# FNet block with a gated MLP on one core: 1.8 MB transfers in halves, y operand sums a pair ahead, the first y unit in a row

## The chip, the core and the metric

The kernel runs on one core of a Trainium2 chip. Its engines are TensorE (PE: matmuls; PEld: loading of their weights), VectorE (DVE), ScalarE (ACT), GpSimd (POOL) and SyncE (SP), which here only issues transfers. The metric is the time on the device in microseconds (us), lower is better.

## The reference

The input x is 2048 x 512, all in float32.

```
xn  = (x - mean) / sqrt(var + 1e-5)                 # per row
a   = xn @ Dre.T ;  b = xn @ Dim.T                  # 512 x 512 each
s   = Sre @ a - Sim @ b                             # 2048 x 2048 each
h   = relu(xn @ w1 + b1) ** 2                       # 512 -> 1792
g   = silu(h @ w2 + b2)                             # 1792 -> 512
out = x + s * g
```

## The kernel before

**Products.** Each float32 operand is split into a high and a low part: ScalarE makes the high part by a rounding copy (L124), VectorE subtracts it from the source to get the low part (L127). A product is three passes, high x high, high x low, low x high. Most matrix products are done by a Strassen-Winograd scheme: of 2 x 2 blocks, sums of blocks are made by VectorE (`sums_b`, `sums_a`, L256 to L268), seven block products numbered 1 to 7 are made on TensorE, and their results are combined. So an operand goes through three stages: load, sums, split.

**Stages, in order.** The order is written out by hand; every engine runs its instructions in that order, and a program-wide tool adds the waits.

1. Layer norm and two chunks (c = 0, 1) of the sequence transform in plain form.
2. Chunks c = 2 to 7 of the sequence transform, 8 steps j each, called "m" (L324). A step takes 42 matmuls of 128 x 256. Its tile u of the transform matrix (512 KB) is loaded four steps ahead into one of three buffers, summed two steps ahead and split one step ahead. The result of a chunk is put together by `combine` (eight "closing" operations, L305) around the start of the next chunk and stored to memory as `pqd`.
3. Y: eight units u = 0 to 7 of 84 matmuls (L702 with operands `wdp`, `yg`), which finish s. Unit u takes the y operands 2u and 2u + 1 (loaded from `pqd`, summed at L262 to L265, split) and the four hidden-transform operands `wdp`. A unit has four PSUM regions A to D. Products 1, 7, 6, 2 of unit u stand between products 5, 4, 3 of unit u - 1. `seed` copies a region to another (ScalarE), `m7`, `c11`, `c12` are ScalarE's copies of results and `c22` (L712), `c21` (L715) VectorE's; `c12` also stores the unit's result y from ScalarE's queue (L741).
4. H: 28 units of 42 matmuls (L702 with `xT`, `w`) of the first MLP product, and O: the second (L808), with the end.

**Side work.** Operands that later stages need are made beside the stages, by generators that advance one stage per call: `go("d2")` runs the next part of d2. Letters: d and v build the hidden-transform and the first two W1 operands and store them (1792 KB each, `wdd` and `w1d`, L375); p loads `wdd` back (L418), k loads `w1d` back (L628); y makes the first y operands 0 to 2; x makes the transposed normalised x (`xT`); m loads rows of the statistics; V, w make further MLP operands; h the operands of O. The tables EARLY (chunk, step), Y_SIDE (unit, two places) and H_SIDE (unit, three places) say where each call stands.

**Queues.** Nearly all loads and the large stores are issued by SP, in program order. An SP instruction that waits for a buffer holds the ones behind it.

The loop of stage 3 before:

```
for u in range(NC):
    n = 2 * u + 3
    ...
    y_sums(n)              # operand 2u+3: the second of unit u+1
    unit.products(1)
    ...
    y_split(n)
    y_load(n + 3)
    ...
    y_sums(n + 1)          # operand 2u+4: the first of unit u+2
    ...
    y_split(n + 1)
    y_load(n + 4)
```

Of the kernel before, what the change touches and what calls it, by code (L numbers as in the profile page):

```python
# [8 lines left out]
F32 = mybir.dt.float32  # L9
# [9 lines left out]
NC = S // CW  # L19
# [20 lines left out]
}  # L40


Y_SIDE = (
    ((), ()),
    (("x0",), ()),
    (("x0",), ()),
    (("x0",), ()),
    (("x0",), ("k0",)),
    (("x1",), ("V2", "V3", "k1")),
    (("x1", "x1", "m1"), ("x1", "V2", "x2")),  # L50
    (("x0", "x0", "V4", "x1", "x1", "V3"), ("x2",)),
)


# [3 lines left out]
    2: (("x2",), ("V4",), ("V6",)),  # L58
    3: (("V5",), ("V5",), ()),
    4: (("V6",), ("V6",), ("w4",)),  # L60
    5: (("x3", "m2"), ("x2",), ("x4",)),
    6: (("x3",), ("x3",), ("x5",)),
    7: (("w4",), ("w4",), ("w5",)),
    8: (("x4",), (), ()),
    9: (("x4",), ("x4",), ("x6",)),
    10: (("w5",), ("w5",), ("w0",)),
    11: (("x5", "m3"), (), ()),
    12: (("x5",), ("x5",), ("x7",)),
    13: (("w0",), ("w0",), ("w1",)),
    14: (("x6",), (), ()),  # L70
    15: (("x6",), ("x6",), ()),
    16: (("x7",), (), ()),
    17: (("x7",), ("x7",), ("h0", "h1")),
    20: (("h0",), (), ()),
    21: (("h1",), (), ()),
# [11 lines left out]
HI, LO = 0, 1  # L87
# [31 lines left out]
def fnet_gated_kernel(ctx, tc, x, xt, ct, wd, w1, w2, b1, b2, out):  # L119
    nc = tc.nc  # L120
    ctx.enter_context(tc.manual_schedule(engines=None))

    def split_hi(hi, lo, src):
        nc.scalar.activation(hi, src, AF.Copy)  # L124

    def split_lo(hi, lo, src):
        nc.vector.tensor_tensor(lo, src, hi.bitcast(F32), op=ALU.subtract)  # L127

    def split(*parts):
        split_hi(*parts)  # L130
        split_lo(*parts)

    def copy(to, src, scale=1.0):
        nc.scalar.activation(to, src, AF.Copy, scale=scale)  # L134
# [12 lines left out]
    PQD = [dram.tile([P, 2, 4, 256], F32, name=f"pqd{c}") for c in range(NC)]  # L147
    WDD = [dram.tile([P, 2, 7, 256], F32, name=f"wdd{n}") for n in range(ND)]
    W1D = {p: dram.tile([P, 2, 7, 256], F32, name=f"w1d{p}") for p in W1_EARLY}
# [8 lines left out]
    def buf(tag, shape, name, dtype=F32):  # L158
        bufs = {"u": 3, "bn": 3, "sm": 3}.get(tag, 1)
        return pool.tile(shape, dtype, tag=tag, bufs=bufs, name=name)  # L160
# [80 lines left out]
    def load_c(c, j, hs=slice(0, 2)):  # L241
        if (c, j) not in raw:
            raw[c, j] = buf("u", [P, 8, CW], f"u{c}_{j}")
        q = slice(2 * hs.start, 2 * hs.stop)
        nc.sync.dma_start(raw[c, j][:, q], ct[c, j, :, q])
# [31 lines left out]
    def step_load(n):  # L277
        if n < len(steps):
            load_c(*steps[n])
        elif n - len(steps) + YFIRST < 2 * 3:  # L280
            y_load(n - len(steps) + YFIRST)

    def step_sums(n):
# [31 lines left out]
    def some(steps_, n):  # L315
        for _ in range(n):
            next(steps_)
# [26 lines left out]
    steps = [(c, j) for c in range(PLAIN, NC) for j in range(NJ)]  # L344
# [3 lines left out]
    def go(*names):  # L348


        for v in names:
            if v[0] == "h" and int(v[1:]) >= NTC * NP:
                continue
            if v not in making:
                making[v] = makers[v[0]](int(v[1:]))
            next(making[v])

    def weight(n, raw_, sums_, to, k, e=None, turn=False):

        if e:  # L360
            e = buf(e, [P, 8, 256], f"{n}rt")
            r, t = e[:, 0:4], e[:, 4:8]
        else:
            r, t = buf(f"pq{k}0", [P, 4, 256], f"{n}r"), buf(f"pq{k}1", [P, 4, 256], f"{n}t")
        nc.sync.dma_start(r, raw_)
        yield
        if turn:
            copy(r[:, I22:I21 + 1], r[:, I22:I21 + 1], -1.0)
        sums_(t, r)
        yield  # L370
        g = buf(f"wd{k}", [P, 2, 7, 256], f"{n}g", F32R)
        split(g[:, HI, 0:3], g[:, LO, 0:3], r[:, 1:4])
        yield
        split(g[:, HI, 3:7], g[:, LO, 3:7], t)
        nc.sync.dma_start(to, g.bitcast(F32))  # L375
        yield

    makers["d"] = lambda n: weight(f"wd{n}", wd[n], sums_b, WDD[n], n % 2, "e" if n == 1 else None, True)
    makers["v"] = lambda n: weight(f"w1{n}", w1[n], sums_w1, W1D[n], n % 2)
# [1 line left out]
    def load_pq(n, x_):  # L381
        nc.sync.dma_start(x_, PQD[n // 2][:, n % 2])

    Y_HOME = ("xc2", "xc3"), ("xc4", "xc5"), ("xc6", "xc7")
    YFIRST = 3
    yop, yraw, WDP = {}, {}, []

    def y_load(n):
        if n < 2 * NC:
            yraw[n] = buf("u", [P, 8, 256], f"yraw{n}")  # L390
            load_pq(n, yraw[n][:, 4:8])

    def y_sums(n):
        if n < 2 * NC:
            sums_rows(yraw[n], yraw[n][:, 4:8], True)

    def y_split(n):
        if n < 2 * NC:
            g = yop[n] = buf(Y_HOME[n // 2 % 3][n % 2], [P, 2, 7, 256], f"yg{n}", F32R)
            split(g[:, HI], g[:, LO], yraw[n][:, 0:7])  # L400
# [14 lines left out]

    def load_wd(n):
        t = buf(("wd0", "wd1", "xc0", "xc1")[n], [P, 2, 7, 256], f"wdp{n}", F32R)
        nc.sync.dma_start(t.bitcast(F32), WDD[n])  # L418
        WDP.append(t)
        yield  # L420

    makers["y"] = y_early
    makers["p"] = load_wd
# [32 lines left out]
    g = plain_parts(0, 1)  # L456
# [7 lines left out]
    for j in range(1, NJ):  # L464
# [15 lines left out]
        g = plain_parts(*order[j + 1])  # L480
# [61 lines left out]
    closing = None  # L542
    for n, s in enumerate(steps):
# [4 lines left out]
        g = part.pop(s)  # L548
# [15 lines left out]
        if closing and j == 1:  # L564
# [3 lines left out]
            closing = None  # L568
        if border:
            step_sums(n + 2)  # L570
        if j == NJ - 1:
            e = buf("e", [P, 2048], f"c{c}")
            closing = combine(chunk_part(e), ms)
# [51 lines left out]

    def load_w1(p):
        t = W1[p] = buf(W1_HOME[p], [P, 2, 7, 256], f"w1_{p}", F32R)
        nc.sync.dma_start(t.bitcast(F32), W1D[p])  # L628
        yield

    def load_w2(p):
        t = W2[p] = buf(W2_HOME[p], [P, 2, 7, 256], f"w2_{p}", F32R)
# [228 lines left out]
        nc.sync.dma_start(at(out[c * TC:(c + 1) * TC], k)[:, cols], z.rearrange("p (k e) -> p k e", e=256))  # L861

    go("m0")
    before = None
    for u in range(NC):
        n = 2 * u + 3
        unit = YUnit(u)
        if not before:
            some(closing, 4)
        y_sums(n)  # L870
        unit.products(1)
        unit.seed("B", "A")
        if before:
            before.c11()
            before.products(5)
            before.c22()
        y_split(n)
        y_load(n + 3)
        if before:
            before.products(4)  # L880
            before.c21()
        else:
            next(closing)
            nc.sync.dma_start(PQD[NC - 1].rearrange("p h k n -> p (h k n)"), e)
        unit.products(7)
        unit.m7()
        y_sums(n + 1)
        go(*Y_SIDE[u][0])
        unit.products(6)
        unit.seed("C", "B")  # L890
        if before:
            before.products(3)
            before.c12()
        y_split(n + 1)
        y_load(n + 4)
        go(*Y_SIDE[u][1])
        unit.products(2)
        before = unit


    for n in range(NTC * NP):
        unit = HUnit(n)
# [19 lines left out]
        before = unit  # L922
# [30 lines left out]
    for n in range(NTC * NP):  # L953
        c, p = divmod(n, NP)
# [34 lines left out]
        if p == NP - 1 and not last:  # L989
            e = buf("e", [P, 4, 512], f"z{c}")  # L990
# [14 lines left out]
    e = buf("u", [P, 4, 512], f"z{c}")  # L1005
# [89 lines left out]
```

## Time and profile before

| | |
|---|---|
| median of 3 runs | 731.75 us (730.14 to 731.95) |
| the profiled execution | 732.29 us |
| its span, first to last instruction | 730.5 us |
| mean granted TensorE clock | 0.992 |
| TensorE busy | 704.0 us |
| VectorE busy | 607.6 us |
| ScalarE busy | 355.8 us |
| moved by DMA | 146.88 MB, 201 GB/s over the span |

In the profile, a row of a timeline gives start, duration, engine, line, operation, output <- input, shapes and count, and in brackets the idle time before it and what ended that. A row of a wait gives the engine and line that waited, what it waited for, the total in us, the number of times and the longest. A group's row gives busy time and mean ns after the bar, then idle time before it. Stage 2 runs from 98 to 343 us, Y from 343 to 434, H to 584.

### The profile page before, as it was taken

How to read it: one execution, taken by the hardware profiler on the slowest of the kernel's cores; microseconds unless marked ns; L12 is line 12 of the kernel's file. 1: busy time of each engine (PE TensorE's matmuls, PEld its weight loads, DVE VectorE, ACT ScalarE, POOL GpSimd, SP SyncE). 2: the span in 40 equal slices, each digit the busy share in tenths (PEclk: the TensorE clock that was granted, in tenths of full speed). 3: DMA queues.
4: the chain of work that ended last, by engine and by line, in shares of the span. 5: the costliest groups of instructions: out<-in, count | busy, mean ns of one | idle time of the engine just before them, and what ended most of it. 6: DMA issues, size and time to landing. Idle time of an engine off the chain costs nothing.

```text
span 730.5 us, 13116 instructions
## 1 busy us (share of the span) xinstructions
PE 704.0 (96%) x5440; PEld 676.3 (93%) x5440; DVE 607.6 (83%) x850; ACT 355.8 (49%) x471; POOL 5.2 (1%) x8
## 2 busy tenths in 40 slices
PE   8999999999998999999899979999999999999996
PEld 6778899999998999999899969999999999999996
DVE  7999779899959887878678768988847878989896
ACT  4446434443432343352443436777778764454441
POOL 0000000000000000000000000000000000101000
PEclk9999999999999999999999989999999999999999
DMA  8435745576583534394454674587435956666644
GB/s 306 170 120 197 293 174 198 185 282 238 174 318 144 217 129 142 106 353 136 130 189 145 239 251 154 190 290 290 174 116 173 347 202 200 169 207 188 217 154 135
DMA packets 47355, 146.88 MB, mean 201 GB/s; under 512 B 4672, under 2 KB 19008, under 8 KB 44352
## 3 DMA queue, kind: packets, MB, share of 16 engines
q1 hardware_dynamic: 40000, 126.13, 50.3%
q10 hardware_dynamic: 6208, 18.88, 6.6%
q0 software_dynamic: 1088, 1.05, 1.1%
q8 instruction: 42, 0.69, 0.4%
q14 instruction: 17, 0.14, 0.1%
HBM read 99.88 MB, written 46.15 MB: 200 GB/s over the span
## 4 chain that ended last, share of the span: by engine, by line
PE 62%; DVE 20%; DMA 7%; ACT 6%; issue 4%; SPq 0%; DVEq 0%; ACTq 0%
PE m L324 18%; PE m_o L808 14%; PE pq_b L339 7%; PE r_B L702 7%; DMA u<-in_ct 5%; PE m_last L808 5%; DVE g L127 4%; PE r_A L702 4%; ACT yg L124 3%; DVE yg L127 2%; PE r_C L702 2%; DVE c L305 2%; PE r_D L702 2%; PE pq_ba L339 1%; PE pq_bc L339 1%
## 5 line engine op out<-in xcount | busy, mean ns | idle before, releaser
L324 PE MATMUL m<-g,xc 128*128 128x256 f32 x2016 | 238.5, 280 | 7.2 <-DVE g L127 7.0
L324 PEld LDWEIGHTS m<-g,xc 128*128 128x128 f32 x2016 | 236.6, 188 | 9.1 <-DVE g L127 8.6
L124 ACT ACTIVATE g<-u 128x1792 fp32r<-128x1792 f32 (+3 forms) x70 | 100.1, 1430 | 155.3 <-PE m L324 79.5
L127 DVE TENSOR_TENSOR g<-u,g 128x1792 fp32r<-128x1792 f32 (+3 forms) x70 | 117.5, 1678 | 22.0 <-ACT g L124 21.8
L808 PE MATMUL m_o<-w,g 128*128 128x256 f32 x882 | 105.8, 282 | 0.4 <-ACT m_o L134 0.4
L808 PEld LDWEIGHTS m_o<-w,g 128*128 128x128 f32 x882 | 105.5, 191 | 0.6 <-ACT m_o L134 0.6
L702 PE MATMUL r_B<-xT,w 128*128 128x256 f32 x504 | 71.3, 284 | 1.6 <-DVE h L712 0.9
L124 ACT ACTIVATE g<-hr 128x1792 fp32r<-128x1792 f32 (+2 forms) x30 | 47.8, 1602 | 49.6 <-PE m_o L808 34.9
L339 PE MATMUL pq_b<-g,xc 128*128 128x512 f32 x240 | 66.7, 397 | 0.8 <-ACT xc L124 0.8
L702 PEld LDWEIGHTS r_B<-xT,w 128*128 128x128 f32 x504 | 64.7, 190 | 3.0 <-DVE h L712 1.7
L127 DVE TENSOR_TENSOR g<-hr,g 128x1792 fp32r<-128x1792 f32 (+2 forms) x30 | 56.7, 1895 | 4.3 <-ACT g L124 4.2
L339 PEld LDWEIGHTS pq_b<-g,xc 128*128 128x128 f32 x240 | 43.8, 187 | 13.8 <-ACT xc L124 2.9
L702 PE MATMUL r_A<-xT,w 128*128 128x256 f32 x336 | 46.3, 285 | 4.8 <-ACT xT L124 3.3
L702 PEld LDWEIGHTS r_A<-xT,w 128*128 128x128 f32 x336 | 42.6, 191 | 5.9 <-ACT xT L124 3.7
L256 DVE TENSOR_TENSOR u<-u 128x512 f32<-128x512 f32 x48 | 32.9, 685 | 13.9 <-DMA u<-in_ct 13.9
L702 PE MATMUL r_B<-wdp,yg 128*128 128x256 f32 x288 | 40.5, 295 | 2.1 <-DVE y L712 2.0
L702 PEld LDWEIGHTS r_B<-wdp,yg 128*128 128x128 f32 x288 | 38.2, 202 | 2.9 <-DVE y L712 2.9
L127 DVE TENSOR_TENSOR yg<-yraw,yg 128x1792 fp32r<-128x1792 f32 x13 | 26.3, 2025 | 17.2 <-ACT yg L124 17.2
L124 ACT ACTIVATE yg<-yraw 128x1792 fp32r<-128x1792 f32 x13 | 22.1, 1701 | 37.6 <-DVE yraw L265 37.6
L808 PE MATMUL m_last<-w,g 128*128 128x256 f32 x294 | 35.3, 282 | 0.0
L808 PEld LDWEIGHTS m_last<-w,g 128*128 128x128 f32 x294 | 35.2, 191 | 0.0
L305 DVE TENSOR_TENSOR c<-m,c 128x512 f32<-128x512 f32 x42 | 27.3, 684 | 2.7 <-DMA yraw<-pqd 2.0
(171 smaller groups left out, 865.4 us busy)
## 6 DMA issues: line engine op xcount, KB each, us to landing
u<-in_ct SPq DMA_DIRECT2D x63, 512.0 KB, 3.6
hd<-h ACTq DMA_DIRECT2D x28, 512.0 KB, 4.0
hr<-hd SPq DMA_DIRECT2D x28, 512.0 KB, 3.6
wdp<-wdd SPq DMA_DIRECT2D x4, 1792.0 KB, 10.7
yraw<-pqd SPq DMA_DIRECT2D x13, 512.0 KB, 4.1
pqd<-c SPq DMA_DIRECT2D x6, 1024.0 KB, 4.3
y<-y ACTq DMA_DIRECT2D x8, 512.0 KB, 5.9
fin<-y SPq DMA_DIRECT2D x16, 256.0 KB, 4.7
```

The lines of the kernel that those rows point to most:

```text
L124: nc.scalar.activation(hi, src, AF.Copy)
L127: nc.vector.tensor_tensor(lo, src, hi.bitcast(F32), op=ALU.subtract)
L256: nc.vector.tensor_tensor(t[:, 0:2], r[:, 0:1].to_broadcast([P, 2, 256]), r[:, 1:3], op=ALU.add)
L305: nc.vector.tensor_tensor(part_(to), m, part_(frm), op=op)
L324: nc.tensor.matmul(ps[:, d], w[:, a_, d * P:(d + 1) * P], halves(mv(b_)), start=first and d == 0 and (a_, b_) == (HI, HI), stop=last and ( ...
L339: nc.tensor.matmul(accs[c][k], w, part[c, j][:, b_, 2 * h:2 * h + 2], start=j == 0 and h == 0 and (a_, b_) == (HI, HI), stop=j == NJ - 1 a ...
L702: nc.tensor.matmul(self.region(REGION[k]), w, mv, start=i == 0 and k in (1, 7), stop=i == len(ops) - 1, skip_group_check=True)
L808: nc.tensor.matmul(m[:, i * 256:(i + 1) * 256], ready[n][:, a_, H_SLOT[a], i * P:(i + 1) * P], W2[p][:, b_, b], start=p == 0 and i == 0 an ...
```

## The change

- The store of a d or v operand is issued in two parts (elements 0 to 2 and 3 to 6 of the seven), each behind its own part of the split; the loads p and k are issued in two halves (high part, low part), each as a call of its own, and EARLY and Y_SIDE place the halves in different steps or units. k0 and k1 stand in units 1 to 4 instead of 4 and 5.
- The side calls y0, y1, y2 move by a step in EARLY.
- At the end of chunk 7 all five remaining closing operations and the store of `pqd` come first; before, the fifth stood behind the split of y operand 3.
- Unit 0 of Y does its seven products in a row. Units 1 to 7 then split the two operands of unit u + 1 and make the sums of the two operands of unit u + 2.
- In Y_SIDE the x, V and m calls are regrouped; in H_SIDE the x calls (and m2, m3) of units 5, 8, 11, 14 and 16 move from the first place to the second, behind `c22` and `c21`.

The number of instructions on PE, DVE and ACT is the same; SP issues twelve more transfers.

```diff
-    (4, 2): ("v1",), (4, 3): ("v1", "y1"), (4, 4): ("p0",), (5, 2): ("p1",), (5, 3): ("y0",), (5, 5): ("y1",),
-    (7, 1): ("p2",), (7, 2): ("p3",), (7, 3): ("y0",), (7, 4): ("y0", "y2", "y1"), (7, 5): ("y1",), (7, 6): ("y2",),
-    (7, 7): ("y2", "y2"),
+    (4, 2): ("v1",), (4, 3): ("v1", "y1"), (4, 5): ("p0",), (4, 6): ("p0",), (5, 2): ("y0",), (5, 3): ("p1",),
+    (5, 4): ("y1",), (5, 5): ("p1",),
+    (7, 1): ("p2",), (7, 2): ("p2", "y0"), (7, 3): ("y0", "y2", "p3"), (7, 4): ("p3", "y1"), (7, 5): ("y1",),
+    (7, 6): ("y2",), (7, 7): ("y2", "y2"),
...
 Y_SIDE = (
     ((), ()),
-    (("x0",), ()),
-    (("x0",), ()),
-    (("x0",), ()),
+    (("x0", "k0"), ()),
     (("x0",), ("k0",)),
-    (("x1",), ("V2", "V3", "k1")),
-    (("x1", "x1", "m1"), ("x1", "V2", "x2")),
-    (("x0", "x0", "V4", "x1", "x1", "V3"), ("x2",)),
+    (("x0",), ("k1",)),
+    (("x0",), ("k1",)),
+    (("x1",), ()),
+    (("V2", "x1", "x1", "m1"), ("x1", "V3", "x2")),
+    (("x0", "x0", "V2", "V4", "V3"), ("x1", "x1", "x2")),
 )
...
-    5: (("x3", "m2"), ("x2",), ("x4",)),
+    5: ((), ("x2", "x3", "m2"), ("x4",)),
-    8: (("x4",), (), ()),
+    8: ((), ("x4",), ()),
-    11: (("x5", "m3"), (), ()),
+    11: ((), ("x5", "m3"), ()),
-    14: (("x6",), (), ()),
+    14: ((), ("x6",), ()),
-    16: (("x7",), (), ()),
+    16: ((), ("x7",), ()),
...
-        split(g[:, HI, 0:3], g[:, LO, 0:3], r[:, 1:4])
-        yield
-        split(g[:, HI, 3:7], g[:, LO, 3:7], t)
-        nc.sync.dma_start(to, g.bitcast(F32))
-        yield
+        for q, src in ((slice(0, 3), r[:, 1:4]), (slice(3, 7), t)):
+            split(g[:, HI, q], g[:, LO, q], src)
+            nc.sync.dma_start(to[:, :, q], g[:, :, q].bitcast(F32))
+            yield
...
-        nc.sync.dma_start(t.bitcast(F32), WDD[n])
         WDP.append(t)
-        yield
+        for i in range(2):
+            nc.sync.dma_start(t[:, i].bitcast(F32), WDD[n][:, i])
+            yield
...
-        nc.sync.dma_start(t.bitcast(F32), W1D[p])
-        yield
+        for i in range(2):
+            nc.sync.dma_start(t[:, i].bitcast(F32), W1D[p][:, i])
+            yield
...
     go("m0")
+    unit = YUnit(0)
+    some(closing, 5)
+    nc.sync.dma_start(PQD[NC - 1].rearrange("p h k n -> p (h k n)"), e)
+    unit.products(1)
+    unit.seed("B", "A")
+    y_sums(3)
+    unit.products(7)
+    unit.m7()
+    unit.products(6)
+    unit.seed("C", "B")
+    y_split(3)
+    y_load(6)
+    unit.products(2)
+    unit.c11()
+    unit.products(5)
+    unit.c22()
+    unit.products(4)
+    unit.c21()
+    unit.products(3)
+    unit.c12()
+    y_sums(4)
+    y_sums(5)
     before = None
-    for u in range(NC):
-        n = 2 * u + 3
+    for u in range(1, NC):
+        n = 2 * u + 2
         unit = YUnit(u)
-        if not before:
-            some(closing, 4)
-        y_sums(n)
+        y_split(n)
+        y_load(n + 3)
         unit.products(1)
         unit.seed("B", "A")
         if before:
             before.c11()
             before.products(5)
             before.c22()
-        y_split(n)
-        y_load(n + 3)
+        y_split(n + 1)
+        y_load(n + 4)
         if before:
             before.products(4)
             before.c21()
-        else:
-            next(closing)
-            nc.sync.dma_start(PQD[NC - 1].rearrange("p h k n -> p (h k n)"), e)
+        y_sums(n + 2)
+        go(*Y_SIDE[u][0])
         unit.products(7)
         unit.m7()
-        y_sums(n + 1)
-        go(*Y_SIDE[u][0])
         unit.products(6)
         unit.seed("C", "B")
         if before:
             before.products(3)
             before.c12()
-        y_split(n + 1)
-        y_load(n + 4)
+        y_sums(n + 3)
         go(*Y_SIDE[u][1])
         unit.products(2)
         before = unit
```

More of the change, by code (lines that the diff above doesn't have):

```diff
@@ L279, in step_load @@
             load_c(*steps[n])
-        elif n - len(steps) + YFIRST < 2 * 3:
+        elif n - len(steps) + YFIRST < 6:
             y_load(n - len(steps) + YFIRST)
```

## The prediction

> **What bounds the kernel now.** I read the engines' busy times first, then TensorE's waits, then the timeline around each wait.
>
> ```profile
> PE 704.0 (96%) x5440; PEld 676.3 (93%) x5440; DVE 607.6 (83%) x850; ACT 355.8 (49%) x471; POOL 5.2 (1%) x8
> PE m L324 <- DVE g L127: 7.0, 8, 1.7
> PE r_A L702 <- ACT xT L124: 3.3, 2, 3.1
> PE r_A L702 <- DVE c L305: 2.7, 1, 2.7
> PE r_B L702 <- DVE y L712: 2.0, 3, 0.7
> ```
>
> TensorE is busy 704.0 of the span's 730.5 us, so a schedule can win only the rest and whatever "busy" hides. The four waits (total, times, longest) are in the three places that the change rewrites. A wait is not its whole price, so each is sized below from start to start.
>
> The profiled execution took 732.3 us, 1.8 outside the span; the median of the runs is 731.75. I sum against 732.3 and take off 0.5 at the end.
>
> **Part 1: the 1.8 MB transfers in halves.**
>
> ```profile
> 214.57 5.17 PE L324 MATMUL m<-g,xc 128*128 128x256 f32 x42 [0.60 <-DVE g L127]
> 221.44 5.19 PE L324 MATMUL m<-g,xc 128*128 128x256 f32 x42 [1.70 <-DVE g L127]
> 227.29 98.93 PE L324 MATMUL m<-g,xc 128*128 128x256 f32 x840 [0.66 <-DVE g L127]
> 203.41 1.43 SPq L418 DMA_DIRECT2D wdp<-wdd  x1
> 217.84 0.69 DVE L256 TENSOR_TENSOR u<-u 128x512 f32<-128x512 f32 x1 [3.33 <-DMA u<-in_ct]
> u<-in_ct SPq DMA_DIRECT2D x63, 512.0 KB, 3.6
> wdp<-wdd SPq DMA_DIRECT2D x4, 1792.0 KB, 10.7
> DMA to landing us min/median/max: 3.4/3.6/10.0
> ```
>
> 840 matmuls in 98.93 us is 0.1178 each, 4.95 for the 42 of a step. The step at 214.57 took 6.87 to the next start, 1.92 lost for an idle time of 1.70; the next took 5.85, 0.90 lost for 0.66. A stop costs its idle time and 0.23, so the eight cost 7.0 + 8 x 0.23 = 8.8 us.
>
> Their cause is in the last five rows. A tile u of the matrix lands in 3.6 us, but in up to 10.0 when it is issued behind a 1792 KB transfer that itself takes 10.7. VectorE, in order, then sits at the sum of that tile (3.33 us at 217.84) with the split that TensorE needs queued behind it. A tile issued in one step is summed two steps later: after the split that frees its buffer (3.8 us into the step: ScalarE's high part 1.7 and VectorE's low part 2.0, the shapes of part 3's rows) there is room of 2 x 4.95 - 3.8 + 1.4 = 7.5 us, the 1.4 being a step less the split (2.0) and the sum (1.5). With halves in different steps, at most 1.0 MB stands ahead of a tile. By the line through 512 KB in 3.6 and 1792 KB in 10.7 (5.5 us per 1000 KB), a tile behind 1000 KB lands in 3.6 + 5.5 = 9.1 if it is issued at once behind it; but the half leaves behind the tile of the step before, some 4 us earlier, which leaves about 5, under 7.5. I take 8.0 of the 8.8 us as gained. Bounds: 4.4 (half the stops stay) to 8.8. The issues themselves cost SP some 0.4 each (the row at 417.86 in part 4), which nothing waits for.
>
> The Trainium skill, "DMA: Bandwidth & Descriptors" (section "Rules for kernel authors"), speaks against this: at least 1 MiB per DMA, with a fixed cost of about 2.0 us each ("Anatomy of one DMA"); by it the twelve added transfers cost 24 us of transfer time, and on the path the sum would stand near 732 again. The rows here give 0.8 us at zero bytes (3.6 - 512 x 0.0055), in a queue that overlaps, and that is the figure of the rival below.
>
> **Part 2: the first y unit in a row, closing sums first.**
>
> ```profile
> 351.31 0.68 DVE L305 TENSOR_TENSOR c<-m,c 128x512 f32<-128x512 f32 x1
> 352.05 1.82 PE L702 MATMUL r_A<-wdp,yg 128*128 128x256 f32 x12 [2.70 <-DVE c L305]
> 353.67 2.76 PE L702 MATMUL r_B<-wdp,yg 128*128 128x256 f32 x12
> 356.23 1.89 PE L702 MATMUL r_C<-wdp,yg 128*128 128x256 f32 x12
> 357.96 1.60 PE L702 MATMUL r_D<-wdp,yg 128*128 128x256 f32 x12
> 362.26 3.03 PE L702 MATMUL r_A<-wdp,yg 128*128 128x256 f32 x24
> 372.29 3.03 PE L702 MATMUL r_A<-wdp,yg 128*128 128x256 f32 x24
> ```
>
> The last closing sum (351.31) stands behind the split of y operand 3 on VectorE; its bank is unit 1's region A, so TensorE idles 2.70 us. Then its clock is low: 36 matmuls from 352.05 to 357.96 took 5.91 us, where 84 in the 10.03 us from 362.26 to 372.29 make 0.1194 each, 4.30 for 36. Lost: 2.70 + 0.2 + 1.6 = 4.5 us.
>
> After, unit 0 alone is 84 x 0.1194 = 10.0 us of matmuls needing only operands 0 and 1. Beside it VectorE does five closing sums (3.3 us), the sums of operand 3 (1.6) and, after ScalarE's 1.7, its split (2.0): done 8.7 us after the unit's start. The new order has a price: product 3 of the unit (8.6 us in) reuses region B, which VectorE reads only behind that split (0.42 more). So it waits 9.1 - 8.6 and a restart: 0.6 us, taken. Operand 5 is likewise ready about when unit 2 wants it: 0.1. Gain 4.5 - 0.7 = 3.8; bounds 2.5 (product 3 waits 2 us) to 4.5.
>
> The Trainium skill, "TensorE: Matmul & The Clock Gate" (section "What's actually happening"), has the clock fall after an idle window of about 3.4 us; by it the 2.70 us gap would not lower the clock and this part would bring 1.6 less. The rows at 353.67 and 356.23 are slow after 2.70, and none is after 1.70, so the measurement decides.
>
> **Part 3: sums a pair ahead.**
>
> ```profile
> 393.62 3.03 PE L702 MATMUL r_A<-wdp,yg 128*128 128x256 f32 x24
> 404.58 3.03 PE L702 MATMUL r_A<-wdp,yg 128*128 128x256 f32 x24
> L127 DVE TENSOR_TENSOR yg<-yraw,yg 128x1792 fp32r<-128x1792 f32 x13 | 26.3, 2025 | 17.2 <-ACT yg L124 17.2
> L124 ACT ACTIVATE yg<-yraw 128x1792 fp32r<-128x1792 f32 x13 | 22.1, 1701 | 37.6 <-DVE yraw L265 37.6
> L262 DVE TENSOR_TENSOR yraw<-yraw 128x512 f32<-128x512 f32 x13 | 8.9, 683 | 0.0
> L265 DVE TENSOR_TENSOR yraw<-yraw 128x256 f32<-128x256 f32 x13 | 5.5, 425 | 0.4
> L609 DVE TENSOR_TENSOR x0e<-x0e,rows 128x1024 f32<-128x1024 f32 x2 | 2.4, 1218 | 0.0
> L712 DVE TENSOR_TENSOR y<-r_B,y 128x256 f32<-128x256 f32 x8 | 3.3, 417 | 0.0
> ```
>
> Late units take 10.96 us against 10.03. In each, VectorE makes the sums, idles while ScalarE makes the high parts (17.2 us over 13 operands), and makes the low parts; c22, which releases product 3, is queued behind. The work itself is 2 x 2.03 (splits) + 2 x 1.53 (sums: 0.68 + 2 x 0.425) + 2 x 0.42 + 1.22 = 9.2 us, under 10.03, so what fails is order. With sums ready a pair ahead, ScalarE runs ahead and VectorE stops only for c22. Gain: three units at 0.93 = 2.8; bounds 1.0 to 3.1.
>
> What is late next: a load of y now has 6.4 us between the split that frees its buffer and its sum (4.1 and 10.5 us after the unit before has ended its product 3, by the durations above), where it had more than a unit. It is 512 KB, 3.6 us alone; behind a half of w it may be 6 to 7. VectorE's slack of 10.03 - 9.2 a unit, and some 1 to 4 us of c22, mostly cover it; unit 1, with the least, would lose 0.8 at a landing of 6. I take 0.8 off; bounds 0 and the price of the last rival.
>
> **Part 4: W1[0] and W1[1] earlier, and the end of the y stage.**
>
> ```profile
> 417.84 0.42 ACTq L741 DMA_DIRECT2D y<-y  x1
> 417.86 0.38 SPq L628 DMA_DIRECT2D w<-w1d  x1
> 425.58 1.59 PE L702 MATMUL r_A<-wdp,yg 128*128 128x256 f32 x12
> 429.12 0.38 ACT L134 ACTIVATE y<-r_D 128x256 f32<-128x256 f32 x1 [9.85 <-DMA y<-y]
> 433.96 2.76 PE L702 MATMUL r_B<-wdp,yg 128*128 128x256 f32 x12
> 436.52 2.61 PE L702 MATMUL r_C<-wdp,yg 128*128 128x256 f32 x12
> 438.96 0.88 PE L702 MATMUL r_D<-xT,w 128*128 128x256 f32 x6
> DMA to landing us min/median/max: 3.2/4.9/11.2
> ```
>
> This is the dearest place. A store of y (417.84) and the 1792 KB of W1[1] (417.86) leave together; the store takes 11.2 us (the maximum in the last row) instead of 4.9. ScalarE must not overwrite that y and stands 9.85 us, with the splits of xT behind it, for which TensorE waits. From 425.58 to 438.96 there are 42 matmuls, 5.0 us of work in 13.38: 8.4 lost, 2.1 of it at the low clock (433.96 to 438.96: 5.00 for 24, against 2.87).
>
> After, W1 is loaded in halves in units 1 to 4, and only loads of 512 KB and the rows are left near the end. A store then has 6.8 us before its buffer is rewritten, against 4.9. In unit 7 the x0 splits come first; the x1 low part is held to the end: VectorE has c22, c21, the x0 low parts (2.1, by 2.03 for 1792 elements), two sums of W1 (3.1), and reaches the x1 low part about 10.2 us after the unit's start, done at 11.2, where the second half of H's first product wants it at 10.7. With restarts I take 1.2 us left, gain 7.2. Bounds 3.7 (a store of 11.2 us again) to 8.4.
>
> **Part 5: the x steps of the H units behind c22.**
>
> ```profile
> 480.52 2.48 DVE L609 TENSOR_TENSOR xr<-xr,rows 128x1024 f32<-128x1024 f32 x2
> 481.65 0.87 PE L702 MATMUL r_B<-xT,w 128*128 128x256 f32 x6
> 483.39 0.98 PE L702 MATMUL r_B<-xT,w 128*128 128x256 f32 x6 [0.88 <-DVE h L712]
> 484.21 1.59 PE L702 MATMUL r_A<-xT,w 128*128 128x256 f32 x12
> ```
>
> In unit 8, x4's two operations (2.48 us) stand ahead of c22, and product 3 waits. From 481.65 to 484.21, 2.56 us for 12 matmuls: 1.1 lost, and gained by the swap, as the next unit's c22 has room for the 2.48. The same move in units 5, 11, 14, 16 I take at nothing: in 5 and 6 VectorE is full, so the wait only moves one unit on. Bounds 0 to 2.
>
> **Sum.** 8.0 + 3.8 + 2.8 - 0.8 + 7.2 + 1.1 = 22.1. 732.3 - 22.1 = 710.2, less 0.5: 709.7 us.
>
> **The rivals.**
> - The transition keeps a wait: the store lands as late as 11.2 us, or the load of W1[3], queued behind four loads of rows, is late for its sum. ScalarE then stands 4.4 us and part 4 brings 3.7 instead of 7.2: 713.2. For: 6.8 us is no wide margin. Against: the median of 4.9. Chance 0.15.
> - Halves queue like wholes: the bytes are the same, so tiles behind them are as late, and part 1 brings 4.4: 713.3. For: at the start of chunk 7 a 1 MB store and both halves follow one another. Against: u's 3.6 median. Chance 0.12. With the rival above: 716.8.
> - VectorE becomes the bound in H: the 8 us of part 4 were also time in which it caught up. If 2.5 us return as waits in units 1 to 8: 712.2. Against: its work per unit is unchanged. Chance 0.06.
> - The fixed cost of twelve more transfers falls on the path: 12 x 0.8 = 9.6 us, 719.3. Against: nothing waits for most of them. Chance 0.03.
> - Slower: the y loads. If one takes longer than 6.4 us, VectorE stands the difference in every one of units 2 to 6. At 13 us, near the 10.7 and 11.2 of transfers that share the queue now, a unit grows from 9.2 + 6.6 = 15.8, that is 5.8 over 10.03: five times is 29 us, giving 739. The point where it cancels the gain is 22.1/5 = 4.4 a unit, a landing of 11.6. For: 6.4 us is the tightest window made. Against: a half has half the queue. Chance 0.04.
>
> **How the numbers follow.** Forecast 0.60, rivals 0.15, 0.12, 0.06, 0.03, 0.04. A difference of 0.3%, 2.2 us, is about what a measurement here can tell from none. All but the last rival lie far below: faster 0.95, slower 0.04, and 0.01 for a mix that cancels. Range: with every bound at its best, 8.8 + 4.5 + 3.1 + 8.4 + 2 = 26.8, the time is 705; I put 704. The top takes in both first rivals together: 717.
>
> **What would show it.** Right: TensorE's wait of m on g near nothing; landings of u under 8 us; y units of 10.0 us; no wait of ScalarE on a store of y; slow rows gone at 353 and 434. In unit 0 a wait of r_B on y of about half a microsecond. Wrong: long waits of VectorE's y sums on loads, SP queued behind halves, or a stop of over 2 us at the first H product. A time above 717 would mean that the halves moved the lateness to the y loads.

## The result

| | before | after |
|---|---|---|
| median | 731.52 us, 4 runs (730.14 to 731.95) | 710.25 us, 4 runs (709.49 to 710.57) |
| ratio | | 0.9711, 95% interval 0.9694 to 0.9728 |
| the profiled execution | 732.29 | 709.49 |
| its span | 730.5 | 707.7 |
| mean granted TensorE clock | 0.992 | 0.999 |

The forecast was 709.7, with a range of 704 to 717. The page after has the same work on the engines; the four loads of wdd, of 1792 KB, have become eight of 896 KB.

```profile
PE 696.0 (98%) x5440; PEld 671.6 (95%) x5440; DVE 607.6 (86%) x850; ACT 357.0 (50%) x471; POOL 5.2 (1%) x8
wdp<-wdd SPq DMA_DIRECT2D x8, 896.0 KB, 7.3
```

TensorE's waits after (engine and line, what it waited for, total us, times, longest). Those of m, of r_A on c and of r_A on ScalarE's xT, which were the three dearest, are gone or under half a microsecond:

```profile
PE r_B L704 <- DVE h L774: 1.3, 1, 1.3
PE m_o L810 <- DVE g L128: 1.0, 1, 1.0
PE r_A L704 <- DVE xT L128: 0.6, 1, 0.6
PE m L325 <- DVE g L128: 0.4, 1, 0.4
```

TensorE's timeline after (start, duration, ..., in brackets the idle time ahead and what ended it):

```profile
100.45 214.97 PE L325 MATMUL m<-g,xc 128*128 128x256 f32 x1831 [0.29 <-DVE plain L537]
335.38 1.58 PE L704 MATMUL r_A<-wdp,yg 128*128 128x256 f32 x12
344.30 1.69 PE L704 MATMUL r_B<-wdp,yg 128*128 128x256 f32 x12 [0.17 <-DVE y L714]
360.48 3.03 PE L704 MATMUL r_A<-wdp,yg 128*128 128x256 f32 x24
370.51 3.03 PE L704 MATMUL r_A<-wdp,yg 128*128 128x256 f32 x24
400.61 3.03 PE L704 MATMUL r_A<-wdp,yg 128*128 128x256 f32 x24
413.56 0.50 PE L704 MATMUL r_A<-xT,w 128*128 128x256 f32 x2 [0.61 <-DVE xT L128]
416.75 0.88 PE L704 MATMUL r_D<-xT,w 128*128 128x256 f32 x6
450.39 0.98 PE L704 MATMUL r_B<-xT,w 128*128 128x256 f32 x6 [1.32 <-DVE h L774]
571.40 95.28 PE L810 MATMUL m_o<-w,g 128*128 128x256 f32 x796 [0.95 <-DVE g L128]
```

1831 matmuls of stage 2 run without a stop, the y units are 10.03 us apart to the end, and the y stage no longer closes with slow rows. Two stops are new: 1.32 us in H at 450.39 and 0.95 us at 571.40 in the second MLP product (m_o and m_last).

The two profiled executions differ by 22.8 us, the medians by 21.3; the profiled one after is the fastest of its four. From start to start, the 22.8 us lie here (each row begins where the one above it ends; a start inside a merged row is half way through it):

| from / to | before | after | gained | forecast |
|---|---|---|---|---|
| m's long row (100.49 before, 100.45 after) / unit 0 | 242.98 | 234.93 | 8.05 | 8.0 |
| unit 0 / unit 2's product 1 | 20.22 | 16.50 | 3.72 | 3.8 |
| / unit 7's product 1 | 53.29 | 50.16 | 3.13 | 2.8 - 0.8 |
| / first r_D of H | 21.98 | 14.71 | 7.27 | 7.2 |
| / first m_o | 142.50 | 140.51 | 1.99 | 1.1 |
| / end of m_last | 143.33 | 144.50 | -1.17 | 0 |
| rest | | | -0.2 | 0 |

### The profile page after: what moved, and what is told of

Its sections match the earlier page's. It is cut to its first block, busy times and chain, and to the rows that moved or that the text cites. A ratio compares the mean times of both kernels' runs of the same rounds, so it can differ in the third digit from the quotient of the medians.

```text
span 707.7 us, 13133 instructions
## 1 busy us (share of the span) xinstructions
PE 696.0 (98%) x5440; PEld 671.6 (95%) x5440; DVE 607.6 (86%) x850; ACT 357.0 (50%) x471; POOL 5.2 (1%) x8
## 4 chain that ended last, share of the span: by engine, by line
PE 90%; DVE 5%; ACT 2%; DMA 1%; issue 1%; ACTq 0%; DVEq 0%; SPq 0%
PE m L325 32%; PE m_o L810 14%; PE r_B L704 13%; PE r_A L704 8%; PE pq_b L340 7%; PE m_last L810 5%; PE r_C L704 4%; PE r_D L704 4%; PE pq_bb L340 1%; PE pq_ba L340 1%; PE pq_bc L340 1%; DMA hr<-hd 1%; DVE g L128 1%; DVE yg L128 1%; DVE c L306 1%
## 5 line engine op out<-in xcount | busy, mean ns | idle before, releaser
L704 PE MATMUL r_B<-xT,w 128*128 128x256 f32 x504 | 69.6, 282 | 1.3 <-DVE h L774 1.3
L704 PE MATMUL r_B<-wdp,yg 128*128 128x256 f32 x288 | 37.5, 283 | 0.2 <-DVE y L714 0.2
L704 PEld LDWEIGHTS r_B<-wdp,yg 128*128 128x128 f32 x288 | 35.6, 190 | 0.6 <-DVE y L714 0.4
```

What stands on the lines that cost most here:

```text
L704: nc.tensor.matmul(self.region(REGION[k]), w, mv, start=i == 0 and k in (1, 7), stop=i == len(ops) - 1, skip_group_check=True)
```

## The experiments

Times are medians; each ratio is to runs of the kernel before on the same chip (0.9711 for the changed kernel).

**Halves in stage 2 alone, on the kernel before.** The edit is the first and last groups of the diff, with Y as it was:

```diff
+ EARLY of the changed kernel
+ stores of d and v in two parts, each behind its split
+ loads p in two halves
```

> The kernel before, with only the stores of d and v and the loads p in halves and the table EARLY of the changed kernel; the y stage as before. Theory (a 1792 KB transfer ahead of a tile u makes the tile late, halves in different steps do not): stage 2, from TensorE's first m matmul to the first y matmul, shrinks from 243.0 to about 235 us, the wait of m on g from 7.0 to under 1 us, the y stage stays: 723.6 us. Rival (the same bytes queue as before, and the gain of stage 2 in the changed kernel came from something else in it): no less than 729.

Measured: 724.72 us, ratio 0.9898 (0.9877 to 0.9918). TensorE's timeline of this kernel:

```profile
100.71 214.73 PE L325 MATMUL m<-g,xc 128*128 128x256 f32 x1831 [0.28 <-DVE plain L537]
343.99 1.90 PE L703 MATMUL r_A<-wdp,yg 128*128 128x256 f32 x12 [2.70 <-DVE c L306]
```

Stage 2 has lost its stops but for one of 0.38 us, and takes 234.69 us from the row at 100.71 to unit 0 (335.40). The stop of 2.70 us in Y is untouched, and from unit 0 to the last row of r_A on wdp Y takes 82.12 us, where it took 82.11 (343.47 to 425.58). So the halves, with the calls of EARLY, are worth 7.4 us by the times, whatever Y does. "DMA: Bandwidth & Descriptors" of the Trainium skill (section "Rules for kernel authors") asks for at least 1 MiB per transfer for the most bandwidth; here parts of 768 to 1024 KB won, since what TensorE paid for was a 512 KB tile that came late behind a large transfer. The 2.0 us that the prediction takes from that page of the Trainium skill ("Anatomy of one DMA") stand there for transfers issued from GpSimd. Those here leave from SP; ten of the twelve added ones are in this run, and it is 7.4 us shorter.

**The changed kernel with whole transfers in stage 2.**

```diff
- stores of d and v in two parts; loads p in halves
+ stores and loads p whole, p at their old steps (y calls stay moved)
```

> The changed kernel with the stores of d and v and the loads p whole again, p0 to p3 at the places of the kernel before; everything else, the y calls of EARLY too, as changed. Theory: the landings of u go up to 10 us again, stage 2 takes 243 instead of 235 us, the y stage stays as changed: 718.3 us. Rival (places of the y calls and not the halves): 710 to 712.

Measured: 715.93, ratio 0.9779 (0.9759 to 0.9798). TensorE's wait in this kernel:

```profile
PE m L325 <- DVE g L128: 4.3, 9, 0.9
```

Nine stops are back, but shorter ones, and stage 2 takes 241.49 us. So 6.6 of the 8.05 us go with the halves and their places, and up to 1.5 with the moved y calls. This second share is not clear of the spread between executions: the three profiles further on that keep stage 2 as before take 242.60, 242.04 and 242.29 us, not 242.98, which leaves 0.6 to 1.1. What was expected of this run was 2.4 us too much, and the y calls explain part of it at most.

**W1[1] one unit earlier, on the kernel before.** One line of Y_SIDE:

```diff
-    (("x0",), ("k0",)),
-    (("x1",), ("V2", "V3", "k1")),
+    (("x0",), ("k0", "k1")),
+    (("x1",), ("V2", "V3")),
```

> The kernel before with one call moved: k1, the whole 1792 KB load of W1[1], stands in unit 4 beside k0 instead of in unit 5 behind V2 and V3. Theory (the store of y beside W1[1] is what held ScalarE for 9.85 us): that wait goes, the end of the y stage loses some 2 us instead of 8.4 because the x splits still stand behind m7, 725.5 us. Rival (the x splits' place makes the stop, whichever transfer is beside it): 730 to 732.

Measured: 724.08, ratio 0.9890 (0.9871 to 0.9909). ScalarE's wait for the store of y, in this kernel:

```profile
ACT y L134 <- DMA y<-y: 2.2, 1, 2.2
```

The wait was 9.85 us, and TensorE no longer stops for xT. Unit 0 to the first r_D of H is 87.12 us, 8.4 less. The prediction's cause of the stall, a store of y beside W1[1], is upheld: with the two parted, the 8.4 us that it priced are gone. ScalarE still waits 2.2 us for a store, and TensorE does not feel it.

**Closing sums first, without unit 0 in a row, on the kernel before.**

```diff
-            some(closing, 4)
+            some(closing, 5)
+            nc.sync.dma_start(PQD[NC - 1]...)
...
-            next(closing)
-            nc.sync.dma_start(PQD[NC - 1]...)
```

> The kernel before with one edit: all five closing operations of chunk 7 and the store of pqd before the split of y operand 3; unit 0 is not in a row. Theory 1 (TensorE waits for the last closing sum, as the wait's row says): the stop of 2.7 us in unit 1 shrinks to the time of the split, and the time falls by 2 to 4.5 us, to 728. Theory 2 (the split of operand 3 is as late as the closing sum, so the order of the two does not matter until unit 1 comes later): operand 3 is split 0.7 us later than before, the stop is now put down to yg and is as long, 731.5 us, the same within 0.3%.

Measured: 731.98, ratio 0.9991 (0.9977 to 1.0006): nothing gained. Its TensorE timeline:

```profile
351.14 0.74 PE L702 MATMUL r_A<-wdp,yg 128*128 128x256 f32 x4 [1.56 <-DVE yg L127]
351.72 1.60 PE L702 MATMUL r_B<-wdp,yg 128*128 128x256 f32 x12
358.31 1.69 PE L702 MATMUL r_B<-wdp,yg 128*128 128x256 f32 x12 [0.70 <-DVE y L712]
359.85 3.03 PE L702 MATMUL r_A<-wdp,yg 128*128 128x256 f32 x24
370.81 3.03 PE L702 MATMUL r_A<-wdp,yg 128*128 128x256 f32 x24
```

The stop of 2.70 us on c becomes one of 1.56 on the split of operand 3, and unit 2 begins 1.5 us sooner after unit 0. But units then take 10.96 us at once (359.85 to 370.81), where the kernel before had one of 10.03 first (362.26 to 372.29): from unit 0 to the last row of r_A on wdp both take 82.11 us. VectorE's pace gives the gain back.

**The last closing sum late again, in the changed kernel** (unit 0 stays in a row).

```diff
-    some(closing, 5)
-    nc.sync.dma_start(PQD[NC - 1]...)
+    some(closing, 4)
...
     y_split(3)
     y_load(6)
+    next(closing)
+    nc.sync.dma_start(PQD[NC - 1]...)
```

> The changed kernel, with its fifth closing sum and the store of pqd put back behind the split of y operand 3; unit 0 stays in a row. Theory A (what the earlier closing sums bought came from the room that unit 0 in a row gives, and unit 1's region A is wanted only 10 us later): the sum is done 0.7 us later than now, long before it is needed; 0 to 0.7 us more than the changed kernel, 710.3 to 711.0, and no stop of product r_A of unit 1. Rival B (the place of the last closing sum is what TensorE's 2.70 us stop hung on, as the prediction said): 2 to 4 us more, 712.5 to 714.5, with a stop of r_A on c.

Measured: 709.75, ratio 0.9716 (0.9701 to 0.9731): no difference from the changed kernel. Its TensorE timeline:

```profile
345.34 1.69 PE L704 MATMUL r_B<-wdp,yg 128*128 128x256 f32 x12 [0.76 <-DVE y L714]
```

The late sum shows only as 0.76 us ahead of product 3 of unit 0, in place of 0.17. No r_A waits for c. So the place of the closing sum, by itself, is worth 0.6 us at most; what took the 2.70 us stop away is that unit 1 comes a whole unit later.

**Each sum right in front of its split, in the changed kernel.**

```diff
-    y_sums(4)
-    y_sums(5)
...
+        y_sums(n)
         y_split(n)
...
+        y_sums(n + 1)
         y_split(n + 1)
...
-        y_sums(n + 2)
...
-        y_sums(n + 3)
```

> The changed kernel, with each sum of a y operand put back right in front of its split (no sums a pair ahead); all else is kept. Theory A (the order on VectorE sets the pace of the y units): units of about 10.9 us again in place of 10.03, some 0.9 in each of six units, about 715.8 (714.5 to 717). Rival B (it is the amount of VectorE's work in a unit, or the loads, that set the pace, and the order is worth little): 710 to 711.5.

Measured: 727.25, ratio 0.9956 (0.9941 to 0.9970). Both theories missed, the nearer one by 11 us. VectorE's timelines show why. Of this kernel, the two splits of a unit:

```profile
397.00 2.02 DVE L128 TENSOR_TENSOR yg<-yraw,yg 128x1792 fp32r<-128x1792 f32 x1 [1.77 <-ACT yg L125]
402.64 2.03 DVE L128 TENSOR_TENSOR yg<-yraw,yg 128x1792 fp32r<-128x1792 f32 x1 [1.77 <-ACT yg L125]
```

Of the kernel before:

```profile
393.48 2.03 DVE L127 TENSOR_TENSOR yg<-yraw,yg 128x1792 fp32r<-128x1792 f32 x1 [1.43 <-ACT yg L124]
399.12 2.03 DVE L127 TENSOR_TENSOR yg<-yraw,yg 128x1792 fp32r<-128x1792 f32 x1 [0.24 <-ACT yg L124]
```

Of the changed kernel:

```profile
383.37 2.03 DVE L128 TENSOR_TENSOR yg<-yraw,yg 128x1792 fp32r<-128x1792 f32 x1
385.90 2.03 DVE L128 TENSOR_TENSOR yg<-yraw,yg 128x1792 fp32r<-128x1792 f32 x1 [0.16 <-ACT yg L125]
```

The prediction's 9.2 us of VectorE work for a unit with an x0 step, and these idle times, give the pace of each: 9.2 + 2 x 1.77 = 12.7 (measured 12.8, from 391.91 to 404.72), 9.2 + 1.43 + 0.24 = 10.9 (measured 10.96), and 9.2 + 0.16 = 9.4, under TensorE's 10.03, which then sets the pace. A unit of the late-sum kernel without an x0 step took 11.3 (404.72 to 416.01), for 8.0 + 3.5. The expectation took the pace of before for any late sum. But the new loop puts both splits in a unit's first half, with nothing between sum and split to cover ScalarE's high part. In the new loop the sums ahead are worth some 17 us: from unit 0 to the first r_D of H this kernel takes 98.80 us, the changed one 81.37. TensorE also stops 3.6 us for xT at the end, which the pace made late.

**The new loop alone, on the kernel before:** unit 0 in a row, closing sums first, sums a pair ahead; transfers whole, all tables old.

```diff
+    unit = YUnit(0)
+    some(closing, 5)
+    ... (unit 0 as in the diff of the change)
-    for u in range(NC):
+    for u in range(1, NC):
...  (the loop as in the diff of the change)
```

> The kernel before with only unit 0 in a row, the closing sums first and the loop with sums a pair ahead; transfers stay whole, the side tables old. Theory A (unit 0 in a row and sums a pair ahead only pay together, since the pace of the later units otherwise gives back what unit 0 gains): units of 10.03 us from unit 1 on, 3.7 and 3.1 us gained, 732 less 6.8: 725 (724 to 726.5), with the wait of ScalarE on the store of y left at the end. Rival B (the end of the stage waits for the loads and stores of y and W1, and gives the gain back there): 729 to 732.

Measured: 717.04, ratio 0.9807 (0.9792 to 0.9822): 14.5 us gained, twice the expectation. TensorE's timeline of this kernel:

```profile
342.80 1.59 PE L702 MATMUL r_A<-wdp,yg 128*128 128x256 f32 x12
357.85 3.03 PE L702 MATMUL r_A<-wdp,yg 128*128 128x256 f32 x24
408.01 3.03 PE L702 MATMUL r_A<-wdp,yg 128*128 128x256 f32 x24
423.05 0.87 PE L702 MATMUL r_D<-xT,w 128*128 128x256 f32 x6
```

From unit 0 to the first r_D of H are 80.25 us, against 95.49 before and 81.37 in the changed kernel: the loop takes away the stall at the end of Y as well, with W1 whole and at its old place. ScalarE's timelines say how. Of the kernel before, behind the copy at 429.12 that waits 9.85 us for the store:

```profile
429.40 1.78 ACT L124 ACTIVATE xT<-x0e 128x768 fp32r<-128x768 f32 x2
431.08 1.78 ACT L124 ACTIVATE xT<-x1e 128x768 fp32r<-128x768 f32 x2
```

Of the loop alone:

```profile
408.63 0.37 ACTq L741 DMA_DIRECT2D y<-y  x1
411.62 1.79 ACT L124 ACTIVATE xT<-x0e 128x768 fp32r<-128x768 f32 x2
413.31 1.79 ACT L124 ACTIVATE xT<-x1e 128x768 fp32r<-128x768 f32 x2
416.39 0.38 ACT L134 ACTIVATE y<-r_D 128x256 f32<-128x256 f32 x1 [1.29 <-DMA y<-y]
```

The new loop has `go(*Y_SIDE[u][0])` ahead of `products(7)` and `m7()`; the old one had it behind. So the splits of xT now stand in front of the copy that waits for the store, and that copy comes up 6.5 us behind the issue of the store (416.39 less 1.29, less 408.63) in place of 1.4. The SP timeline of the same kernel has W1[1] leaving 2.9 us ahead of the store, not beside it:

```profile
405.76 0.42 SPq L628 DMA_DIRECT2D w<-w1d  x1
```

That the loop ends the stall is shown; how much each of these two does of it, no run parts.

**The changed kernel with the old Y_SIDE and W1 whole.**

```diff
- Y_SIDE of the changed kernel, W1 loaded in halves in units 1 to 4
+ Y_SIDE of before, W1[0] in unit 4 and W1[1] in unit 5, whole
```

> The changed kernel with the old table Y_SIDE and W1[0] and W1[1] loaded whole, in units 4 and 5 again; the halves of stage 2, the new loop, the closing order and H_SIDE stay. Theory A (the new loop alone already takes the store of y and the load of W1[1] apart, so moving W1 earlier and cutting it adds nothing to it): 709.0, from 708 to 710.5, with W1[1] leaving some 3 us ahead of a store, a wait of ScalarE on it of 1 to 3 us, and no stop of r_A on xT. Rival B (the prediction's part 4: the earlier W1 is what ended the stall): the stall of the end of the stage is back, 714 to 718.

Measured: 707.86, ratio 0.9672 (0.9649 to 0.9696), 707.46 to 708.63: no stall, and if anything faster than the changed kernel. Its TensorE timeline:

```profile
335.86 1.59 PE L703 MATMUL r_A<-wdp,yg 128*128 128x256 f32 x12
416.14 0.87 PE L703 MATMUL r_D<-xT,w 128*128 128x256 f32 x6
```

80.28 us again, 1.1 less than in the changed kernel, whose new table puts V2, V4 and V3 in front of the x1 splits and so makes the stop of 0.61 at 413.56. Theory A holds in the time, but not in two details: W1[1] left 1.2 us ahead of a store, not 3, and ScalarE waited 6.3 us for a store, not 1 to 3, in an earlier unit, where TensorE kept its 10.03. Once the loop is new, the earlier W1 and its halves bring nothing that the times show.

**Both halves of W1 together, at nearly the new places.** Each W1 operand is still loaded in two transfers, but one directly behind the other.

```diff
-    (("x0", "k0"), ()),
-    (("x0",), ("k0",)),
-    (("x0",), ("k1",)),
-    (("x0",), ("k1",)),
+    (("x0",), ()),
+    (("x0",), ("k0", "k0")),
+    (("x0",), ()),
+    (("x0",), ("k1", "k1")),
```

> The changed kernel with both halves of W1[0] issued together in unit 2 and both of W1[1] in unit 4, in place of one half in each of units 1 to 4. Theory A (in the Y stage the place of these loads counts, not their halving: VectorE has the sums ready a pair ahead, which covers a late tile of y): within 1 us of the changed kernel, 709.5 to 711.5, with waits of the y sums on loads of under 2 us in all. Rival B (whole transfers hold up the y loads, as the prediction's last rival had it): landings of y of 9 us and more, and 2 to 6 us more, 712.5 to 716.

Measured: 709.48, ratio 0.9717 (0.9699 to 0.9736). VectorE's wait for the y loads, in this kernel:

```profile
DVE yraw L263 <- DMA yraw<-pqd: 3.6, 3, 2.8
```

The sums wait 3.6 us in all, more than the 2 allowed, though no y load took over 6.9 us. TensorE's units stay at 10.03 but for one of 10.62, at 390.58. Its timeline shows a stop there that hangs on ScalarE, which had stood 7.00 us for a store of y:

```profile
393.93 1.70 PE L704 MATMUL r_B<-wdp,yg 128*128 128x256 f32 x12 [0.33 <-ACT r_C L135]
```

The end of Y is 1.2 us longer than in the changed kernel (82.59 against 81.37), and the median does not show it. So the time holds theory A; issuing the halves of W1 apart is worth about a microsecond at most.

**The old H_SIDE in the changed kernel.**

```diff
-    8: ((), ("x4",), ()),
+    8: (("x4",), (), ()),
... (units 5, 11, 14 and 16 alike)
```

> The changed kernel with the old table H_SIDE: the x calls of units 5, 8, 11, 14 and 16 stand in the first place again, ahead of c22. Theory A (the 2.0 us that the H stage gained come from this table alone): about 712.3 (711.7 to 713), with stops of r_B on h in units 8, 11, 14 or 16. Rival B (the H stage gained because ScalarE and VectorE leave the transition less late): about 710.5, with H as long as in the changed kernel, 140.5 us. The prediction had 1.1 us for it, from unit 8 alone: 711.4.

Measured: 711.37, ratio 0.9737 (0.9721 to 0.9754). In its TensorE timeline the stop of unit 8 is back:

```profile
462.33 0.98 PE L704 MATMUL r_B<-xT,w 128*128 128x256 f32 x6 [0.88 <-DVE h L714]
477.80 0.98 PE L704 MATMUL r_B<-xT,w 128*128 128x256 f32 x6 [0.16 <-DVE h L714]
```

H takes 143.5 us in that execution against 140.5, but it is the slowest of its four, and one stop of 0.78 us, at 544.34, is in a unit that the table does not touch. The medians differ by 1.1 us, the ratios by 1.9, and the two ratios' intervals overlap. The table is worth 1 to 2 us.

**A version with three more edits, and then with two of them.** In unit 7 the x1 splits go ahead of the V parts; one more entry in ACT_PAIR moves work of H unit 4 from VectorE to ScalarE; the first of the two versions also loads w2 in halves.

```diff
-    (("x0", "x0", "V2", "V4", "V3"), ("x1", "x1", "x2")),
+    (("x0", "x0", "x1", "x1", "V2", "V4"), ("V3", "x2")),
...
-ACT_PAIR = (7, 10, 13, 15, 17, 18, 19, 20, 26)
+ACT_PAIR = (4, 7, 10, 13, 15, 17, 18, 19, 20, 26)
... (first version only: w2 in two halves, l4 and l5 spread over H units 25 to 27 and O step 0)
```

> The changed kernel with three more edits of the same kind: in unit 7 of Y the two x1 splits stand ahead of the V parts; in H unit 4 two of the operations move from VectorE to ScalarE (one more entry in ACT_PAIR), ahead of the 1.3 us stop at h; the last two loads of w2 (1792 KB) are issued in halves in different places, ahead of the hr load that waits for a store. Theory A (each of the stops left is a wait of the kinds found so far): 0.76 at H's first product, some 1 at unit 5's or 6's c22, about 1 at the start of the second MLP product, together 2 to 2.8: 707.5 to 708.3. Rival B (the store is late for another reason than the whole w2 loads and VectorE stays full at H's start): 709.5 to 710.5.

Measured: 706.63, ratio 0.9677 (0.9658 to 0.9697), a little more than theory A allowed.

> The changed kernel with two of the three edits of the improved version: the x1 splits ahead of the V parts in unit 7, and one more entry in ACT_PAIR; the loads of w2 stay whole. Theory A: these two bring 1.8 of its 3.2 us, so about 708.2, and executions in which the store hd lands late still have the stop of m_o. Rival B (halving the loads of w2 brings nothing that the times show): 706.5 to 707.2.

Measured: 707.41, ratio 0.9677 (0.9661 to 0.9693), so the same: halving w2 brings nothing that these times show (each interval is over 1 us either way). TensorE's timeline of the second one has the stop in H halved:

```profile
447.89 0.98 PE L704 MATMUL r_B<-xT,w 128*128 128x256 f32 x6 [0.61 <-DVE h L774]
```

Both lie some 3 us under the changed kernel. In the profile of the second one 1.1 of it is the end of Y (80.28 us from unit 0 to r_D) and 0.7 this stop; the rest is in stages that these edits don't touch, 0.8 in the second MLP product, where the stop at 571.40 is absent, and 0.6 in stage 2.

## Why the prediction was right, and where its sum hid an error

**Part 1** holds: forecast 8.0, measured 8.05, and 7.4 by itself. VectorE's waits for tiles u, of the kernel before and of the changed one, show the mechanism:

```profile
DVE u L256 <- DMA u<-in_ct: 13.9, 8, 3.3
DVE u L257 <- DMA u<-in_ct: 0.7, 2, 0.4
```

The rival that halves queue like wholes is out: with the transfers whole again VectorE waits 11.4 us. The sign that the prediction gave, landings of u under 8 us, does not tell the two apart. From the view of tile u after:

```profile
DMA to landing us min/median/max: 3.3/3.7/8.4
```

The slowest landing is 9.4 us with the halves alone, where TensorE has lost its stops, and 9.2 with whole transfers in the changed kernel, where nine are back. So it seems to matter which tile is late, not how late the latest is. Two things stay open: up to 1.5 of the 8 us can be the moved y calls, and no run parts the halving from the new places of the p calls.

**Part 2** came out at 3.72 against 3.8. TensorE did idle 2.70 for the last closing sum, as it said, but the step that failed is that this sum has to come first. With the sum early and unit 0 not in a row, the split itself is waited for (1.56), and the 1.5 us won are given back by the later pace. With the sum late and unit 0 in a row, the time is that of the changed kernel. Unit 0 in a row does it, and the place of the sum is worth 0.6 us at most. The stop ahead of product 3 was foreseen at 0.6 and is 0.17 idle, 0.33 from start to start.

**Part 3**: forecast 2.8 less 0.8, measured 3.13. The order on VectorE is the cause, as said: idle time for ScalarE's high part plus 9.2 us of work reproduces two measured paces, and puts the third under TensorE's own. The sum missed 0.34 us of a fourth late unit (372.29 to 382.66), and the 0.8 for late y loads was not paid: they landed in at most 7.0 us, about as feared, but VectorE waited 0.3 us for them in all (from its waits, after):

```profile
DVE yraw L263 <- DMA yraw<-pqd: 0.3, 2, 0.2
```

Parts 2 and 3 were added as if each stood alone, and they don't: closing sums first without sums ahead brought nothing, since the later pace took it back.

**Part 4**: forecast 7.2, measured 7.27, and the cause of the stall was right (moving W1[1] alone brought 8). The step that failed is what removes it in this change: the prediction gave it to the earlier W1. Old places and whole loads under the new loop are 1.1 us shorter here. Two things each take the stall away, W1[1] moved and the new loop, and their gains don't add. ScalarE's timeline after shows the splits of x0e ahead of the copy, which now waits only for TensorE:

```profile
404.23 1.79 ACT L125 ACTIVATE xT<-x0e 128x768 fp32r<-128x768 f32 x2
407.98 0.38 ACT L135 ACTIVATE y<-r_D 128x256 f32<-128x256 f32 x1 [1.96 <-PE r_D L704]
```

The 1.2 us left over was sized rightly, and its cause too: the x1 low part comes late (413.56).

One sign of being right was not met: "no wait of ScalarE on a store of y". From ScalarE's waits, after:

```profile
ACT y L135 <- DMA y<-y: 7.7, 2, 4.3
```

The slowest of these stores still takes 9.7 us (11.2 before), more than the 6.8 of room that the prediction counted on. Both waits, at 370.92 and 379.71, come in units where a half of W1 is under way and no split of xT stands behind the copy, so TensorE keeps its 10.03. That is close: in the profile of the old-H_SIDE version, whose Y stage is the changed kernel's, such a wait of 6.90 us reached TensorE and made one unit 10.79 us long, as the 7.00 us did with both halves together. The first rival's late store is thus still there, at a place where it costs little.

**Part 5**: forecast 1.1, measured 1.99 start to start and 1 to 2 with the table undone. "In 5 and 6 the wait only moves one unit on" holds for the place, not for the size: the stop was 0.35 us in unit 5 (466.67 before) and is 1.32 in unit 6 (450.39), and from unit 4's r_D to unit 7's it is 16.9 us in place of 16.3. Units 11, 14 and 16, taken at nothing, make up for it with one to four tenths each.

**Not foreseen**: 1.17 us lost in the second MLP product. VectorE stood 6.99 us for the load hr, which SP held back until a store hd had landed (the first row from VectorE's timeline, then SP's wait, then the landings of the hd stores, after):

```profile
567.79 0.69 DVE L263 TENSOR_TENSOR hr<-hr 128x512 f32<-128x512 f32 x1 [6.99 <-DMA hr<-hd]
```

```profile
SPq L674 <- DMA hd<-h: 17.2, 3, 11.2
```

```profile
DMA to landing us min/median/max: 2.6/4.0/12.1
```

These stores are under way beside the last whole loads of w2. The same instructions gave no stop of m_o in the profiles of the closing-late, W1-together and old-Y_SIDE versions, so it seems to belong to the execution; what makes those transfers 10.9 us in one and 9.2 in another (medians of the two w2 loads, changed kernel and closing-late version) stays open.

By the runs the gain is built of two parts that add: 7.4 us from halves and EARLY, 14.5 from the loop. With 1 to 2 of H_SIDE that makes 23 to 24, which the version with old Y_SIDE has: 731.61 - 707.86 = 23.75. The new Y_SIDE costs some of it; its trace shows 1.1 us. So the forecast's sum was right section by section, while part 4 named the wrong edit for it, and part 2 named two where one does it. That the total came so close, 709.7 against 710.25, is partly luck: parts 3 and 5 brought 2.0 us more than forecast, and the unforeseen stop took 1.2 back.

## What to carry to other kernels

Price a stall by start-to-start times, and then ask which edits would each remove it alone: gains of edits that remove the same stall don't add, and a correct sum doesn't show which edit earned it. An engine's pace in a loop is its work plus the idle time that its order leaves for its partner; compute that sum for the old and the new order before trusting either. Look at what stands behind a copy that waits for a store: where ready work can go ahead of that copy, try it before reshaping transfers.

## What the runs showed of the hardware

The two loads of w2 (1792 KB) and the stores beside them differ by over a microsecond between kernels whose instructions there are the same (changed kernel, closing-late, W1-together, old Y_SIDE): the median of the two loads is 9.2 to 10.9 us, the slowest hd store 9.7 to 12.1. Only the execution with the slowest of them, the changed kernel's, has the stop of 0.95 us in the second MLP product.

A wait of 2.70 us was followed by slow matmuls (the prediction's rows at 353.67 and 356.23): the granted TensorE clock was 0.50 from 353.67 to 356.23 and 0.81 from there to 357.96. After 1.56 us, at 351.14 in the closing-first version, the next twelve matmuls took 1.60 (351.72 there), and the clock stayed at 1.00.
